# Two token blocks take the feed-forward in two half passes, partial sums in DRAM, and the batches are paired differently

## The chip, the cores and the metric

The kernel runs on one core of a Trainium2 chip. Its time is device time in microseconds (us), the median of several executions. The engines are PE (TensorE, matrix products; PEld is its loading of weights), DVE (VectorE), ACT (ScalarE), POOL (GpSimd) and SP (SyncE). SP computes nothing here: it issues every DMA, in one queue and in program order.

## The reference

Attention with a relative-position bias over 4 batches, 8 heads, 576 positions and a head size of 64, and behind it a gated feed-forward on the 2304 tokens that come out:

```python
scores = scale * np.matmul(q, k.transpose(0, 1, 3, 2))
x = (psi_rel / psi_i)[..., None]           # logs of distance and of position
bias = np.maximum(x @ w1 + b1, 0.0) @ w2   # 32 hidden units, one value per head
scores = scores + bias.transpose(2, 0, 1)[None, :, :, :]
attn = softmax(scores)                     # over the last axis
x = np.matmul(attn, v)                     # then (B*S, H*D) = (2304, 512)
h = x @ w_in                               # (2304, 2048)
g = h * (1.0 / (1.0 + np.exp(-h)))
out = g @ w_out                            # (2304, 512)
```

`w_in` and `w_out` arrive as 64-bit floats, all else as 32-bit.

## The kernel before

**Attention.** The bias depends on the head and the two positions alone. It is made once, in 36 tiles, and stored to DRAM in five pieces (`bias_d`), one for each chunk of 128 query rows (the fifth has 64). Two heads make a pair (`hp`), so a batch has 4 pairs and 5 chunks. For each head and chunk PE makes the scores (lines 561, 552), DVE adds the bias and takes the row maximum in one instruction (line 568, with a short read of its accumulator behind it), ACT takes the exponential (line 575), PE transposes (line 584), DVE or ACT evicts (lines 590 and 595, through the helper on lines 270 and 272), and one `pv` group of PE multiplies by the values (line 483). Batch 0 goes chunk by chunk, 20 `pv` groups. The other batches go pair by pair with two visits each, chunks 0 and 1 and then 2 to 4: 24 more groups, so the last is the 44th. A visit pair needs 9 maxima of line 568 and gives 2 `pv` groups. The loop `for some in ((1, 2), (3,))` sets who shares bias loads: the dictionary `biases` is cleared once per pair of heads and tuple, so batches 1 and 2 read each piece of the bias once for both, and batch 3 reads all of it again.

**Feed-forward.** The 2304 tokens are 6 blocks of 384 (`TB`), the 2048 columns 16 tiles of 128 (`NF`). Block 0 needs batch 0 alone, block 1 needs batches 0 and 1. `split_x` loads a block's attention output (`x_d`) and the reciprocals of its row sums (`rec_d`), multiplies (line 614, on DVE or POOL) and splits each of four tiles into a high part and a rest (lines 618 and 622), which go through PE as three products. A step `ff_step` is one column tile: 12 matmuls of 384 columns into `hp` (line 633), tanh on ACT (line 638), the gate on DVE (line 642), a split again (lines 646 and 650), and 9 matmuls of 512 columns that add into three banks `acc` (line 656). Behind 16 steps the banks are halved into SBUF (lines 681 and 683) and stored to `out`.

**Weights.** Block 0 meets each column tile first. `prepare` loads a 64-bit tile of 512 KB, and `narrow` makes 32-bit floats of it: one operation on ACT (line 356) and four on DVE (lines 360, 364, 369, 374). Then it is split, by ACT (line 387) and by POOL or DVE (line 391). There are 32 such tiles, a `w_in` and a `w_out` for each step. The split `w_in` is stored to DRAM (`win_d`, line 666) and loaded again by the blocks 1 to 5 (line 671); `w_out` stays in SBUF.

**Order.** All of it is recorded as operations with an assumed cost and a due time, and the class `Plan` writes one order for each engine from these: at each moment a free engine takes the ready operation with the earliest due time whose buffers are to be had. So attention and feed-forward are woven on every engine, and each engine then runs its list strictly in that order. `LEAD` is how long after batch 0 block 0 falls due, `STEP` the spacing of the steps while attention still runs (10 us in block 0, 7 in the next), `DF` the spacing behind it.

Of the kernel before, what the change touches and what calls it, by code (L numbers as in the profile page):

```python
# [8 lines left out]
F32 = mybir.dt.float32  # L9
# [3 lines left out]
ALU = mybir.AluOpType  # L13
# [4 lines left out]
DM, DFF = 512, 2048  # L18
NT = B * S
NF = DFF // 128  # L20
NC = DM // 128
TB = 384
NBLK = NT // TB
# [4 lines left out]
T0, DC, B1, BD, GAP0, DF, WU = 16.0, (4.5, 3.0), 36.0, 2.6, 2.0, 4.3, 24  # L28


PACE, LEAD, STEP = (1.1, 1.6), 30.0, (10.0, 7.0)


def f(ap):
    return ap.bitcast(F32)
# [180 lines left out]
def attention_moe_kernel(ctx: ExitStack, tc: tile.TileContext, q, k, v, small, w_in, w_out, lut, ident_d, out):  # L216
    nc = tc.nc
    V, A, G, T, SP = nc.vector, nc.scalar, nc.gpsimd, nc.tensor, nc.sync
# [10 lines left out]
    dpool = ctx.enter_context(tc.tile_pool(name="dram", bufs=1, space=DRAM))  # L229
# [9 lines left out]
    win_d = [dpool.tile([128, 2 * DM], F32, name=f"win_d{i}") for i in range(NF)]  # L239
    win_b = [Buf(None) for _ in range(NF)]  # L240
    x_d = [dpool.tile([128, NC, TB], F32, name=f"x_d{i}") for i in range(NBLK)]
    x_b = [Buf(None) for _ in range(NBLK)]

    rec_d = dpool.tile([NC, 2, NBLK * TB], F32, name="rec_d")
# [32 lines left out]
    def op(kind, where, prio, reads=(), writes=(), shy=6.0):  # L277
        def add(fn):
            plan.op(kind, where, prio, fn, reads, writes, shy=shy)
            return fn  # L280
        return add

    def load(kind, prio, writes, fn, bytes, reads=(), plain=False):
        plan.op(kind, ("SP", 0.52 if plain else 0.7), prio, fn, reads, writes, bytes)
# [92 lines left out]
    def prepare(t0, src):  # L377

        w, wr = buf("w", [128, DM]), buf("G", [128, 2, DM], F32R)
        if wide:  # L380
            narrow(t0, w, src)
        else:
            load("ld_w32", t0 - 6, [w], lambda e: SP.dma_start(out=tl(w), in_=src), 262144)

        @op("split_hi", ("ACT", 0.62), t0 + 0.5, reads=[w], writes=[(wr, 0)])
        def _(e):
            copy(e, tl(wr)[:, 0, :], tl(w))

# [235 lines left out]

    PAIRS = ((0, 0), (0, 1), (1, 0))

    def ff_step(blk, fi, xs, wr, acc, t0):
        hp, th, gg = bank("h", 1), buf("th", [128, TB]), buf("M", [128, 2, TB], F32R)
        for cc in range(NC):
            @op("h_mm", ("PE", 0.53), t0 + 0.01 * cc, reads=[xs[cc], wr], writes=[hp])  # L630
            def _(e, cc=cc):
                for m, (x, y) in enumerate(PAIRS):
                    T.matmul(out=tl(hp)[:, 0:TB], lhsT=tl(wr)[:, x, 128 * cc:128 * cc + 128], rhs=tl(xs[cc])[:, y, :],  # L633
                             start=(cc + m == 0), stop=(cc == NC - 1 and m == 2))

        @op("tanh", ("ACT", 0.5), t0 + 2.3, reads=[hp], writes=[th])
        def _(e):
            A.activation(out=tl(th), in_=tl(hp)[:, 0:TB], func=AF.Tanh, scale=0.5)  # L638

# [12 lines left out]
        for i in range(3):  # L652
            @op("out_mm", ("PE", 0.7), t0 + 2 * DF + 0.01 * i, reads=[gg, wo[fi]], writes=[acc[i]])
            def _(e, i=i):
                for m, (x, y) in enumerate(PAIRS):
                    T.matmul(out=tl(acc[i]), lhsT=tl(gg)[:, x, 128 * i:128 * i + 128], rhs=tl(wo[fi])[:, y, :],  # L656
                             start=(fi == 0 and m == 0), stop=(fi == NF - 1 and m == 2))

    def ff_block(blk, t0, step):
        xs = split_x(blk, t0 - 8)  # L660
        acc = [bank("acc", 1) for _ in range(3)]
        for fi in range(NF):
            t = t0 + step * fi
            if blk == 0:
                wr = prepare(t - 5, w_in[fi])
                load("st_in", t - 1, [win_b[fi]], lambda e, wr=wr, fi=fi: SP.dma_start(out=win_d[fi], in_=f(tl(wr).rearrange("p a n -> p (a n)"))), 524288, reads=[wr])
                if wo[fi] is None:
                    wo[fi] = prepare(t - 2, w_out[128 * fi:128 * fi + 128, :])
            else:
                wr = buf("G", [128, 2, DM], F32R)  # L670
                load("ld_in", t - 8, [wr], lambda e, wr=wr, fi=fi: SP.dma_start(out=f(tl(wr).rearrange("p a n -> p (a n)")), in_=win_d[fi]), 524288, reads=[win_b[fi]])
            ff_step(blk, fi, xs, wr, acc, t)
        for i in range(3):
            ob = buf("M", [128, DM])
            t = t0 + step * (NF - 1) + 2 * DF + 3
            cuts = [(0, DM)] if blk < NBLK - 1 or i < 2 else [(0, DM // 2), (DM // 2, DM)]
            for x, y in cuts:
                @op("out_ev", {"ACT": 0.18 + (y - x) * 0.00083, "DVE": 0.15 + (y - x) * 0.00104}, t, reads=[acc[i]], writes=[(ob, x)])
                def _(e, i=i, ob=ob, x=x, y=y):
                    if e == "ACT":  # L680
                        A.activation(out=tl(ob)[:, x:y], in_=tl(acc[i])[:, x:y], func=AF.Copy, scale=0.5)
                    else:
                        V.tensor_scalar_mul(out=tl(ob)[:, x:y], in0=tl(acc[i])[:, x:y], scalar1=0.5)

                row = TB * blk + 128 * i
                load("st_out", t + 1, [], lambda e, ob=ob, row=row, x=x, y=y: SP.dma_start(
                    out=out[row:row + 128, x:y], in_=tl(ob)[:, x:y]), 512 * (y - x), reads=[(ob, x)])


    kv, vs, sq = {}, {}, {}  # L690
    t = T0
# [11 lines left out]

    t1 = t + LEAD
    t2 = t1 + NF * STEP[0]
    for some in ((1, 2), (3,)):
        for hp in range(4):
            biases.clear()
            for b in some:
                pace = PACE[t > t2]  # L710
                kv, vs, sq = keys(b, hp, t), values(b, hp, t), sums(t)
                for chunks in ((0, 1), (2, 3, 4)):
                    t = visit(b, hp, chunks, kv, vs, sq, t, pace)
                factors(b, hp, sq, t)
    wo = [None] * NF
    for blk in range(NBLK):
        step = STEP[0] if blk == 0 else STEP[1] if t1 < t else DF
        ff_block(blk, t1, step)
        t1 += NF * step

    def warm_up():

# [65 lines left out]
```

## Time and profile before

| what | us |
|---|---|
| median of 3 runs (735.53 to 736.71) | 736.17 |
| the profiled execution's own time | 736.04 |
| its span | 734.3 |
| PE busy | 712.6 |
| DVE busy | 421.0 |
| ACT busy | 389.4 |
| POOL busy | 281.4 |

The own time is 1.7 us over the span, which is what lies ahead of the first and behind the last instruction. Matmuls overlap in the records, so a PE shown as busy may still give less than it can; what a piece of PE work costs at the least is read from an unbroken run of it in the chain of waits. Records of DVE overlap too: the instructions of one stretch, summed, give some 0.06 us per instruction more than DVE's busy time there.

### The profile page before, as it was taken

The numbers are of one execution on the slowest core, as the hardware profiler recorded it, in microseconds if no ns is written. First come the engines' busy times: TensorE is split into PE (matmuls) and PEld (weight loads), VectorE is DVE, ScalarE is ACT, GpSimd is POOL, SyncE is SP. The second block draws the span as 40 slices with busy tenths as digits, with TensorE's granted clock in tenths as the row PEclk, the third lists the DMA queues.
The fourth block names the chain that finished last, engine by engine and source line by source line (L and its number), as shares of the span: only waits on it lengthen the run. The fifth ranks groups of instructions, "written<-read, shape, count | busy, mean of one in ns | idle before, by whom it ended". The sixth has DMA issues, their size and how long they took to land.

```text
span 734.3 us, 13019 instructions
## 1 busy us (share of the span) xinstructions
PE 712.6 (97%) x4642; PEld 590.1 (80%) x4642; DVE 421.0 (57%) x862; ACT 389.4 (53%) x820; POOL 281.4 (38%) x277
## 2 busy tenths in 40 slices
PE   9899999999999999989999999999999999999997
PEld 4376698677777787778888888899998999999996
DVE  6999968999999999996553544213211221211111
ACT  8899968886786777765443454222222232222222
POOL 5464524474746445573122251123223322422221
PEclk9999999999999999999999999999999999999999
DMA  6998899898584594879856567736454644346001
GB/s 195 372 315 270 277 310 359 278 289 297 191 290 157 203 303 149 272 257 311 293 165 224 168 217 241 263 115 196 148 162 153 186 150 152 125 136 195 1 0 44
DMA packets 68384, 154.77 MB, mean 211 GB/s; under 512 B 9056, under 2 KB 24032, under 8 KB 68320
## 3 DMA queue, kind: packets, MB, share of 16 engines
q1 hardware_dynamic: 68320, 153.94, 63.7%
q8 instruction: 37, 0.61, 0.4%
q14 instruction: 27, 0.22, 0.1%
HBM read 125.12 MB, written 28.79 MB: 210 GB/s over the span
## 4 chain that ended last, share of the span: by engine, by line
PE 46%; issue 7%; DVE 3%; POOL 2%; DMA 1%; ACT 0%; POOLq 0%; DVEq 0%; ACTq 0%
PE psum L633 18%; PE psum L656 18%; PE psum L483 3%; PE psum L561 3%; PE psum L584 3%; POOL M L275 2%; DVE G L568 1%; DVE w L369 1%; DMA G<-in_k_dram 1%; PE psum L552 1%; DVE M L275 0%; DVE w L374 0%; DVE th L642 0%; DVE M L272 0%; DVE w L360 0%
## 5 line engine op out<-in xcount | busy, mean ns | idle before, releaser
L633 PE MATMUL psum<-M,G 128*128 128x384 f32 x1152 | 238.8, 339 | 1.0 <-POOL M L275 0.8
L656 PE MATMUL psum<-G,M 128*128 128x512 f32 x864 | 238.0, 397 | 1.2 <-DVE M L275 0.9
L633 PEld LDWEIGHTS psum<-M,G 128*128 128x128 f32 x1152 | 203.4, 188 | 16.6 <-POOL M L275 1.0
L275 POOL TENSOR_TENSOR M<-th,M 128x384 fp32r<-128x384 f32 x82 | 84.9, 1035 | 272.0 <-ACT M L270 189.3
L642 DVE SCALAR_TENSOR_TENSOR th<-th,psum 128x384 f32<-128x384 f32 x96 | 53.0, 552 | 216.4 <-ACT th L638 216.4
L656 PEld LDWEIGHTS psum<-G,M 128*128 128x128 f32 x864 | 156.7, 188 | 22.2 <-DVE M L275 1.6
L575 ACT ACTIVATE G<-G,sm 128x576 f32<-128x576 f32 (+1 forms) x144 | 111.8, 777 | 53.6 <-DVE sm L568 52.3
L638 ACT ACTIVATE th<-psum 128x384 f32<-128x384 f32 x96 | 47.1, 491 | 161.1 <-PE psum L633 160.0
L568 DVE CUSTOM_DVE_ANT_0 G<-psum,G 128x576 f32<-128x576 f32 (+1 forms) x144 | 106.5, 758 | 27.9 <-PE psum L561 15.5
L584 PE MATMUL psum<-ident,G 128*128 128x128 f32 x656 | 93.5, 276 | 5.7 <-DVE sm L568 3.3
L561 PE MATMUL psum<-G,M 128*128 128x288 f32 x512 | 90.9, 310 | 4.9 <-DVE sm L568 3.5
L584 PEld LDWEIGHTS psum<-ident,G 128*128 128x128 f32 x656 | 75.3, 141 | 23.0 <-issue 4.8
L561 PEld LDWEIGHTS psum<-G,M 128*128 128x128 f32 x512 | 73.9, 190 | 19.7 <-issue 6.7
L483 PE MATMUL psum<-pt,M 128*64 128x128 f32 (+3 forms) x880 | 87.5, 346 | 1.6 <-DVE sm L568 0.8
L483 PEld LDWEIGHTS psum<-pt,M 128*64 128x64 f32 x880 | 52.1, 137 | 30.7 <-issue 6.8
L270 ACT ACTIVATE pt<-psum 128x512 f32<-128x512 f32 (+3 forms) x111 | 59.4, 551 | 28.1 <-PE psum L584 27.0
L275 POOL TENSOR_TENSOR M<-M 64x256 fp32r<-64x256 f32 (+3 forms) x40 | 48.6, 1217 | 57.9 <-DVE M L272 21.0
L270 ACT ACTIVATE M<-th 128x384 fp32r<-128x384 f32 x81 | 42.3, 523 | 40.9 <-DVE th L642 40.0
L272 DVE COPY pt<-psum 128x512 f32<-128x512 f32 (+3 forms) x81 | 45.4, 571 | 21.8 <-PE psum L584 19.1
L275 POOL TENSOR_TENSOR G<-w,G 128x512 fp32r<-128x512 f32 x25 | 35.6, 1425 | 23.8 <-ACT G L270 19.9
L275 POOL TENSOR_TENSOR G<-G 128x576 fp32r<-128x576 f32 x21 | 32.2, 1540 | 29.6 <-PE psum L334 9.6
L326 ACT ACTIVATE G<-lut_sb,cb 128x528 f32<-128x528 f32 (+16 forms) x71 | 41.6, 662 | 0.0
(55 smaller groups left out, 574.1 us busy)
## 6 DMA issues: line engine op xcount, KB each, us to landing
G<-win_d SPq DMA_DIRECT2D x80, 512.0 KB
G<-bias_d SPq DMA_DIRECT2D x48, 576.0 KB
bias_d<-G SPq DMA_DIRECT2D x36, 295.5 KB
G<-in_k_dram SPq DMA_DIRECT2D x16, 576.0 KB
G<-in_w_in_dram SPq DMA_DIRECT2D x16, 512.0 KB
G<-in_w_out_dram SPq DMA_DIRECT2D x16, 512.0 KB
win_d<-G SPq DMA_DIRECT2D x16, 512.0 KB
M<-in_v_dram SPq DMA_DIRECT2D x16, 320.0 KB
```

The costliest lines, as they stand in the source:

```text
L270: A.activation(out=out, in_=in_, func=AF.Copy)
L272: ENG[e].tensor_copy(out=out, in_=in_)
L275: ENG[e].tensor_tensor(out=out, in0=in0, in1=f(in1), op=ALU.subtract)
L483: T.matmul(out=tl(o)[x, 0:w], lhsT=tl(vs)[:, (s + 1) % 5 * 128 + 64 * a:(s + 1) % 5 * 128 + 64 * a + 64], rhs=tl(pt)[:, s + 5 * a if s < 4 ...
L561: T.matmul(out=s[:, hf, 0:288], lhsT=tl(qs)[:, x0 + 128 * a:x0 + 128 * a + 128], rhs=tl(part)[:, S * a + 288 * hf:S * a + 288 * hf + 288], ...
L568: V.tensor_tensor_reduce(out=mine(p, a).rearrange("p (a n) -> p a n", a=2), in0=tl(sps[a]).rearrange("p (a n) -> p a n", a=2)[:, :, 0:widt ...
L575: A.activation(out=mine(p, a), in_=mine(p, a), func=AF.Exp, scale=-1.0, bias=tl(sm)[:, i + a:i + a + 1], accum_out=tl(sq)[:, 2 * c + a:2 * ...
L584: T.transpose(out=tl(tp)[:, 128 * s:128 * s + 128], in_=tl(p)[:, 128 * (s0 + s):128 * (s0 + s) + 128], identity=ident)
L633: T.matmul(out=tl(hp)[:, 0:TB], lhsT=tl(wr)[:, x, 128 * cc:128 * cc + 128], rhs=tl(xs[cc])[:, y, :], start=(cc + m == 0), stop=(cc == NC - ...
L638: A.activation(out=tl(th), in_=tl(hp)[:, 0:TB], func=AF.Tanh, scale=0.5)
L642: V.scalar_tensor_tensor(out=tl(th), in0=tl(th), scalar=1.0, in1=tl(hp)[:, 0:TB], op0=ALU.add, op1=ALU.mult)
L656: T.matmul(out=tl(acc[i]), lhsT=tl(gg)[:, x, 128 * i:128 * i + 128], rhs=tl(wo[fi])[:, y, :], start=(fi == 0 and m == 0), stop=(fi == NF - ...
```

## The change

Blocks 0 and 1 take the columns in two halves, by turns: block 0 with tiles 0 to 7, block 1 with tiles 0 to 7, block 0 with 8 to 15, block 1 with 8 to 15. A first half ends by storing its three halved accumulators to DRAM (`part_d`), a second half loads them (line 682 of the changed kernel) and adds them in its last eviction, on DVE alone. Each half calls `split_x` for itself. The second half of block 0 prepares its weight tiles with due times up to 40 us (`AHEAD`) earlier than its steps, and loads `w_in` back from `win_d` like the others. Blocks 2 to 5 are as they were. Of the attention, batch 1 now goes alone and batches 2 and 3 share the bias loads.

```diff
+AHEAD = 40.0
...
+    part_d = [dpool.tile([TB, DM], F32, name=f"part_d{i}") for i in range(2)]
+    part_b = [Buf(None) for _ in range(2)]
...
-                             start=(fi == 0 and m == 0), stop=(fi == NF - 1 and m == 2))
+                             start=(fi == fs[0] and m == 0), stop=(fi == fs[-1] and m == 2))
...
-        for fi in range(NF):
-            t = t0 + step * fi
-            if blk == 0:
-                wr = prepare(t - 5, w_in[fi])
-                load("st_in", t - 1, [win_b[fi]], lambda e, wr=wr, fi=fi: SP.dma_start(out=win_d[fi], in_=f(tl(wr).rearrange("p a n -> p (a n)"))), 524288, reads=[wr])
-                if wo[fi] is None:
-                    wo[fi] = prepare(t - 2, w_out[128 * fi:128 * fi + 128, :])
-            else:
+        for n, fi in enumerate(fs):
+            t = t0 + step * n
+            ahead, fresh = AHEAD if part else 0.0, wo[fi] is None
+            if wo[fi] is None:
+                wr = prepare(t - 5 - ahead, w_in[fi])
+                load("st_in", t - 1 - ahead, [win_b[fi]], lambda e, wr=wr, fi=fi: SP.dma_start(out=win_d[fi], in_=f(tl(wr).rearrange("p a n -> p (a n)"))), 524288, reads=[wr])
+                wo[fi] = prepare(t - 2 - ahead / 2, w_out[128 * fi:128 * fi + 128, :])
+            if part or not fresh:
                 wr = buf("G", [128, 2, DM], F32R)
...
+            if part:
+                load("ld_part", t - 12, [ob], lambda e, ob=ob, at=at: SP.dma_start(out=tl(ob), in_=at), 262144, reads=[(part, i)])
...
+                    if part:
+                        V.scalar_tensor_tensor(out=tl(ob)[:, x:y], in0=tl(acc[i])[:, x:y], scalar=0.5, in1=tl(ob)[:, x:y], op0=ALU.mult, op1=ALU.add)
...
+                if len(fs) < NF and not part:
+                    load("st_part", t + 1, [(part_b[blk], i)], lambda e, ob=ob, at=at: SP.dma_start(out=at, in_=tl(ob)), 262144, reads=[(ob, x)])
...
-    for some in ((1, 2), (3,)):
+    for some in ((1,), (2, 3)):
...
-    for blk in range(NBLK):
-        step = STEP[0] if blk == 0 else STEP[1] if t1 < t else DF
-        ff_block(blk, t1, step)
-        t1 += NF * step
+    low, high = range(NF // 2), range(NF // 2, NF)
+    runs = [(0, low, STEP[0], None), (1, low, STEP[1], None), (0, high, STEP[0], part_b[0]), (1, high, STEP[1], part_b[1])]
+    for blk, fs, step, part in runs + [(blk, range(NF), None, None) for blk in range(2, NBLK)]:
+        step = step or (STEP[1] if t1 < t else DF)
+        ff_block(blk, t1, step, fs, part)
+        t1 += len(fs) * step
```

The plan weaves anew from there on, so each engine's order moves. The three places below are those that the prediction speaks of. Most lines of the changed kernel are numbered 3 higher than before (483 is 486, 568 is 571, 633 is 636, 656 is 659, 459 is 462).

On PE, behind the 23rd `pv` group (the first row of the first piece). Before, the first feed-forward step (line 633) starts there:

```order
L483 MATMUL psum<-pt,M 64x256 x10
L584 MATMUL psum<-ident,G 128x128 x5
L561 MATMUL psum<-G,M 128x288 x4
L633 MATMUL psum<-M,G 128x384 x3
L552 MATMUL psum<-G,M 128x320 x2
L552 MATMUL psum<-G,M 128x256 x2
L552 MATMUL psum<-G,M 128x320 x2
L552 MATMUL psum<-G,M 128x256 x2
L633 MATMUL psum<-M,G 128x384 x9
```

In the changed kernel it starts behind the 24th, which is the fourth row from the end here:

```order
L587 MATMUL psum<-ident,G 128x128 x5
L564 MATMUL psum<-G,M 128x288 x4
L587 MATMUL psum<-ident,G 128x128 x4
L564 MATMUL psum<-G,M 128x288 x4
L528 MATMUL psum<-ident,sq 128x128
L587 MATMUL psum<-ident,G 128x128 x5
L486 MATMUL psum<-pt,M 64x320 x10
L587 MATMUL psum<-ident,G 128x128 x4
L636 MATMUL psum<-M,G 128x384 x12
L587 MATMUL psum<-ident,G 128x128 x5
```

The first step moved behind one more `pv` group, and both groups belong to batch 1 now. From the 26th to the 36th group more feed-forward stands between two groups than before: ahead of the 36th, 19 steps of line 633 against 17.

On DVE, around the 79th to the 81st maximum of line 568, in the fifth visit pair behind batch 0. Before, weight tiles (`w`, lines 360, 364, 369, 374) stand between the maxima:

```order
L369 SCALAR_TENSOR_TENSOR w<-G,w 128x512
L568 ISA G,sm<-psum,G 128x576
L568 ISA sm 128x1
L374 SCALAR_TENSOR_TENSOR w<-G,w 128x512
L568 ISA G,sm<-psum,G 128x576
L568 ISA sm 128x1
L360 TENSOR_SCALAR w<-w 128x512
L272 COPY pt<-psum 128x4x128
L364 TENSOR_SCALAR w<-w 128x512
L369 SCALAR_TENSOR_TENSOR w<-G,w 128x512
L272 COPY pt<-psum 128x5x128
L642 SCALAR_TENSOR_TENSOR th<-th,psum 128x384
```

Now there are none here; the eviction of a partial sum (line 693) and the tokens of the next half (`xp`) stand in their place:

```order
L571 ISA G,sm<-psum,G 128x576
L571 ISA sm 128x1
L617 TENSOR_TENSOR xp<-xp 128x384
L571 ISA G,sm<-psum,G 128x576
L571 ISA sm 128x1
L275 CAST M<-xp 128x384
L571 ISA G,sm<-psum,G 128x576
L571 ISA sm 128x1
L693 TENSOR_SCALAR M<-psum 128x512
L275 COPY xo<-psum 128x256
L275 COPY pt<-psum 128x4x128 x2
L275 CAST M<-xp 128x384
```

The weight tiles moved behind: before, all 32 are done ahead of the last maximum of the 36th `pv` group (the 108th); now 27 are done there, and the 32nd stands right behind the last maximum of the 38th group (the 117th).

On SP, where the last visits of batch 0 end. Before, the loads of the 64-bit weights and of `k` stand there with one piece of the bias (`G<-bias_d`):

```order
L352 DMA G<-in_w_out_dram 128x1024
L352 DMA G<-in_w_in_dram 128x1024
L497 DMA x_d_121<-xo 128x128
L352 DMA G<-in_w_out_dram 128x1024
L532 DMA rec_d<-rt 4x2x128
L534 DMA rec_d<-rt 2x1x64
L406 DMA G<-in_k_dram 128x1152
L459 DMA G<-bias_d_99 128x2x576
```

In the changed kernel:

```order
L462 DMA G<-bias_d_101 128x2x576
L462 DMA G<-bias_d_102 128x2x576
L355 DMA G<-in_w_in_dram 128x1024
L535 DMA rec_d<-rt 4x2x128
L500 DMA x_d_121<-xo 128x64
L537 DMA rec_d<-rt 2x1x64
L355 DMA G<-in_w_out_dram 128x1024
L409 DMA G<-in_k_dram 128x1152
L462 DMA G<-bias_d_99 128x2x576
L500 DMA x_d_121<-xo 128x64
L459 DMA G<-bias_d_103 64x576 x2
```

The bias of batch 1's second pair of heads moved in, which batch 2's visits used to put off: up to the 23rd `pv` group there are 40 issues of bias loads against 33.

## Rows read from the trace of the kernel before

**Rows 1.** The page: busy time of the engines over the whole span (its part 1), and from its part 2 the busy tenths of PE, of DVE and of the DMA engines in 40 slices of 18.4 us.

```profile
PE 712.6 (97%) x4642; PEld 590.1 (80%) x4642; DVE 421.0 (57%) x862; ACT 389.4 (53%) x820; POOL 281.4 (38%) x277
...
PE   9899999999999999989999999999999999999997
...
DVE  6999968999999999996553544213211221211111
...
DMA  6998899898584594879856567736454644346001
```

**Rows 2.** Busy time by stretch (the windows view). Columns: stretch in us, its length, then busy us (and instructions) of PE, PEld, DVE, ACT and POOL, the granted TensorE clock as a share of full speed, the mean busy share of the 16 DMA engines, GB/s.

```profile
90.00:145.90 55.90, 53.37 (x542) 45.62 (x532) 45.76 (x117) 42.85 (x98) 22.10 (x34) 1.00 0.97 319
145.90:219.80 73.90, 68.82 (x447) 56.25 (x446) 72.21 (x129) 56.52 (x118) 41.16 (x37) 1.00 0.79 266
219.80:334.60 114.80, 108.69 (x713) 88.55 (x712) 108.99 (x199) 84.28 (x179) 62.29 (x53) 1.00 0.68 229
334.60:464.40 129.80, 129.80 (x821) 109.78 (x820) 65.42 (x145) 58.23 (x128) 34.50 (x36) 1.00 0.71 231
361.60:464.40 102.80, 102.80 (x644) 87.26 (x643) 48.33 (x109) 44.75 (x100) 26.57 (x31) 1.00 0.64 208
464.40:734.30 269.90, 265.73 (x1332) 238.25 (x1331) 49.06 (x92) 67.34 (x132) 73.48 (x73) 1.00 0.41 131
```

**Rows 3.** The timeline of PE at three places: where the 23rd, the 36th and the 38th `pv` group (line 483) start. Columns: start us, us, engine, line, operation, tiles, shapes, count. A group is 10 instructions of the program and 20 of the trace.

```profile
145.85 2.38 PE L483 MATMUL psum<-pt,M 128*64 128x256 f32 x20
...
334.64 1.57 PE L483 MATMUL psum<-pt,M 128*64 128x320 f32 x10
...
361.62 2.91 PE L483 MATMUL psum<-pt,M 128*64 128x320 f32 x20
```

**Rows 4.** The chain of work that ended last, in order of time, inside the attention stage and just behind it: start us, us, what. Each row is a run of matmuls without a break, so its second column is what that piece costs on a PE that never waits.

```profile
334.71 2.84 PE psum L483 x20
337.56 1.14 PE psum L584 x9
338.69 1.06 PE psum L561 x8
...
345.97 2.31 PE psum L483 x20
...
351.68 1.06 PE psum L552 x8
...
475.93 2.10 PE psum L633 x12
478.03 2.08 PE psum L656 x9
```

**Rows 5.** DVE's instructions from 145.9 to 334.6 us by line and tile. Columns: line, operation, tiles, shapes, count, then busy us and mean ns of one, then DVE's idle time just before them and what ended it.

```profile
L568 DVE CUSTOM_DVE_ANT_0 G<-psum,G 128x576 f32<-128x576 f32 (+1 forms) x61 | 45.1, 755 | 1.7 <-PE psum L561 1.1 <-ACT G L575 0.3
L369 DVE SCALAR_TENSOR_TENSOR w<-G,w 128x512 uint32<-128x512 uint32 x29 | 30.0, 1035 | 0.4
L374 DVE SCALAR_TENSOR_TENSOR w<-G,w 128x512 uint32<-128x512 uint32 x30 | 27.0, 899 | 0.1
L360 DVE TENSOR_SCALAR w<-w 128x512 f32<-128x512 f32 x28 | 20.0, 713 | 0.8 <-ACT w L356 0.7
L364 DVE TENSOR_SCALAR w<-w 128x512 uint32<-128x512 uint32 x28 | 18.0, 642 | 0.2
...
L642 DVE SCALAR_TENSOR_TENSOR th<-th,psum 128x384 f32<-128x384 f32 x16 | 8.7, 547 | 2.0 <-ACT th L638 2.0
L275 DVE TENSOR_TENSOR G<-w,G 128x512 fp32r<-128x512 f32 x6 | 7.6, 1273 | 0.2 <-ACT G L270 0.2
L568 DVE DVE_READ_ACCUMULATOR2_ANT sm<- 128x1 f32 x61 | 4.8, 79 | 0.0
...
L275 DVE TENSOR_TENSOR M<-th,M 128x384 fp32r<-128x384 f32 x4 | 3.9, 996 | 0.0
...
L272 DVE CAST M<-th 128x384 fp32r<-128x384 f32 x6 | 2.9, 483 | 0.0
...
L272 DVE COPY xo<-psum 128x256 f32<-128x256 f32 (+1 forms) x3 | 1.3, 437 | 0.0
L275 DVE TENSOR_TENSOR M<-M 64x704 fp32r<-64x704 f32 x1 | 1.0, 1029 | 0.0
...
L614 DVE TENSOR_TENSOR xp<-xp 128x384 f32<-128x384 f32 x1 | 0.5, 549 | 0.0
```

**Rows 6.** The same stretch and engine with different shapes kept apart: two rows that the view before has merged.

```profile
L272 DVE COPY pt<-psum 128x512 f32<-128x512 f32 x9 | 6.1, 681 | 0.9 <-PE psum L584 0.9
...
L272 DVE COPY pt<-psum 128x640 f32<-128x640 f32 x7 | 5.7, 812 | 0.0
```

**Rows 7.** Two of DVE's four weight operations over the whole run (the view of one source line): count, shortest/median/longest ns, first and last start in us, shape.

```profile
L360 DVE TENSOR_SCALAR w<-w x32: 406/422/1920, 127.3 to 314.2; 128x512 f32<-128x512 f32 x32
...
L369 DVE SCALAR_TENSOR_TENSOR w<-G,w x32: 674/692/2218, 130.4 to 318.1; 128x512 uint32<-128x512 uint32 x32
```

**Rows 8.** What DVE waited for on the DMA side (the list of waits, whole run): us in total, times, longest us.

```profile
DVE xp L614 <- DMA xp<-x_d: 7.5, 4, 2.5
```

**Rows 9.** POOL's two operations on the tokens of a feed-forward block, from 145.9 to 334.6 us, columns as in rows 5.

```profile
L614 POOL TENSOR_TENSOR xp<-xp 128x384 f32<-128x384 f32 x7 | 8.8, 1264 | 4.8 <-DMA xp<-x_d 4.3 <-DMA xp<-rec_d 0.4
L275 POOL TENSOR_TENSOR M<-xp,M 128x384 fp32r<-128x384 f32 x7 | 8.3, 1197 | 2.1 <-DVE M L272 1.4 <-ACT M L270 0.4 <-PE psum L584 0.3
```

More of the change, by code (lines that the diff above doesn't have):

```diff
@@ L625, in attention_moe_kernel, with ff_step @@
     PAIRS = ((0, 0), (0, 1), (1, 0))
[L627 removed]
+    def ff_step(fs, fi, xs, wr, acc, t0):
         hp, th, gg = bank("h", 1), buf("th", [128, TB]), buf("M", [128, 2, TB], F32R)
@@ L656, in _, with ff_block @@
                     T.matmul(out=tl(acc[i]), lhsT=tl(gg)[:, x, 128 * i:128 * i + 128], rhs=tl(wo[fi])[:, y, :],
-                             start=(fi == 0 and m == 0), stop=(fi == NF - 1 and m == 2))
-    def ff_block(blk, t0, step):
+                             start=(fi == fs[0] and m == 0), stop=(fi == fs[-1] and m == 2))
+    def ff_block(blk, t0, step, fs, part=None):
         xs = split_x(blk, t0 - 8)
         acc = [bank("acc", 1) for _ in range(3)]
-        for fi in range(NF):
-            t = t0 + step * fi
-            if blk == 0:
-                wr = prepare(t - 5, w_in[fi])
-                load("st_in", t - 1, [win_b[fi]], lambda e, wr=wr, fi=fi: SP.dma_start(out=win_d[fi], in_=f(tl(wr).rearrange("p a n -> p (a n)"))), 524288, reads=[wr])
-                if wo[fi] is None:
-                    wo[fi] = prepare(t - 2, w_out[128 * fi:128 * fi + 128, :])
-            else:
+        for n, fi in enumerate(fs):
[6 more added lines that the diff above has]
+            if part or not fresh:
@@ L670, in ff_block @@
                 wr = buf("G", [128, 2, DM], F32R)
                 load("ld_in", t - 8, [wr], lambda e, wr=wr, fi=fi: SP.dma_start(out=f(tl(wr).rearrange("p a n -> p (a n)")), in_=win_d[fi]), 524288, reads=[win_b[fi]])
-            ff_step(blk, fi, xs, wr, acc, t)
+            ff_step(fs, fi, xs, wr, acc, t)
+        t = t0 + step * (len(fs) - 1) + 2 * DF + 3
         for i in range(3):
             ob = buf("M", [128, DM])
-            t = t0 + step * (NF - 1) + 2 * DF + 3
+            at = part_d[blk][128 * i:128 * i + 128, :] if len(fs) < NF else None
+            if part:
+                load("ld_part", t - 12, [ob], lambda e, ob=ob, at=at: SP.dma_start(out=tl(ob), in_=at), 262144, reads=[(part, i)])
@@ L676, in ff_block @@
             cuts = [(0, DM)] if blk < NBLK - 1 or i < 2 else [(0, DM // 2), (DM // 2, DM)]
             for x, y in cuts:
-                @op("out_ev", {"ACT": 0.18 + (y - x) * 0.00083, "DVE": 0.15 + (y - x) * 0.00104}, t, reads=[acc[i]], writes=[(ob, x)])
+                @op("out_ev", ("DVE", 0.15 + (y - x) * 0.00104) if part else {"ACT": 0.18 + (y - x) * 0.00083, "DVE": 0.15 + (y - x) * 0.00104},
+                    t, reads=[acc[i]], writes=[(ob, x)])
                 def _(e, i=i, ob=ob, x=x, y=y):
-                    if e == "ACT":
+                    if part:
+                        V.scalar_tensor_tensor(out=tl(ob)[:, x:y], in0=tl(acc[i])[:, x:y], scalar=0.5, in1=tl(ob)[:, x:y], op0=ALU.mult, op1=ALU.add)
+                    elif e == "ACT":
@@ L685, in ff_block @@
                 row = TB * blk + 128 * i
-                load("st_out", t + 1, [], lambda e, ob=ob, row=row, x=x, y=y: SP.dma_start(
-                    out=out[row:row + 128, x:y], in_=tl(ob)[:, x:y]), 512 * (y - x), reads=[(ob, x)])
+                if len(fs) < NF and not part:
+                    load("st_part", t + 1, [(part_b[blk], i)], lambda e, ob=ob, at=at: SP.dma_start(out=at, in_=tl(ob)), 262144, reads=[(ob, x)])
+                else:
+                    load("st_out", t + 1, [], lambda e, ob=ob, row=row, x=x, y=y: SP.dma_start(
+                        out=out[row:row + 128, x:y], in_=tl(ob)[:, x:y]), 512 * (y - x), reads=[(ob, x)])
     kv, vs, sq = {}, {}, {}
```

## The prediction

> **What bounds the kernel now.** I read the page first. PE is busy 712.6 of 734.3 us [rows 1], so time can be won only where that busy time is not full: the busy tenths show DVE at 8 to 9 in the first 18 slices and falling from there, PE without a gap behind them. The windows say it more sharply [rows 2]. From 145.9 to 334.6 us DVE is busy 72.21 + 108.99 = 181.2 of 188.7 us; from 334.6 on PE is busy in every microsecond and DVE in half of them. I chose these two cuts because `pv` groups start there, the 23rd and the 36th [rows 3]: just behind the 23rd the feed-forward begins, and at the 36th the last of the 32 weight tiles has been made. The chain of waits prices PE's work where nothing interrupts it [rows 4]: 12 matmuls of line 633 take 2.10 us, 9 of line 656 2.08, 8 of line 561 or of line 552 1.06, 9 transposes 1.14, a `pv` group 2.31 (256 columns) or 2.84 (320). By these, PE's order holds 170 us of work between the 23rd and the 36th group (192 of line 633, 153 of 656, 212 of 561, 48 of 552, 264 of 584, 13 groups), so PE could have been done 18 us sooner. That is all there is to win. What fills DVE there is attention's maxima, 45.1 us, and the weight tiles, 30.0 + 27.0 + 20.0 + 18.0 = 95.0 us [rows 5].
>
> So the end is DVE's queue up to the last weight tiles, and then PE's work that is left. Before: 334.6 us and 734.3 - 334.6 = 399.7 us.
>
> **The change part by part.** The matmuls are the same in number. Weight tiles too: 32, one each. What changes is how much PE work stands in the order beside DVE's work. In the changed order DVE's heavy stretch ends at the 38th group (its 117th maximum), with the 32nd tile right behind it; there are two numbers to work out, DVE's work up to there and PE's work from there.
>
> *DVE.* I counted its order between the 49th maximum (the last that the 23rd group needs) and the 108th before, the 117th after. Each mean is reduced by 0.06 us, since records overlap by that much. Added [rows 5, 6]: 9 maxima with their accumulator reads, 9 x (0.755 + 0.079 - 0.12) = 6.4; evictions for the transposed weights, 6 of 512 and 5 of 640 elements, 6 x 0.62 + 5 x 0.75 = 7.5; 8 casts of 384, 8 x 0.42 = 3.4; 5 evictions of `pv`, 1.9; subtractions on line 275, 3 of 384, 2 on `M` of 64 partitions, and 2 fewer on weights, 2.8 + 1.9 - 2.4 = 2.3; 4 gates, 1.9; two block ends and two multiplications of tokens (line 614) at about 0.5 each, 2.0. Removed: five of the weight operations (2, 1, 1, 1 of lines 360, 364, 369, 374), 3.7. The sum is +21.7, so 181.2 + 21.7 = 202.9 us of DVE work.
>
> *DVE's pace.* It was busy 97.7% of the first part of its stretch (72.21 of 73.9) and 94.9% of the second (108.99 of 114.8) [rows 2]; in the second PE was busy 94.7%, in the first 93.1%. The changed stretch has more PE work beside the same DVE work, which is nearest to the second part, so I take 94.9%: 202.9 / 0.949 = 213.8 us. The 38th group then starts at 145.9 + 213.8 = 359.7 us, where before the 36th started at 334.6 and the 38th at 361.6 [rows 3].
>
> *PE from there.* Behind the start of the 38th group the changed order has less than the old one behind its 36th: 48 matmuls of line 633 (8.4 us), 36 of 656 (8.3), 24 of 561 (3.2), 8 of 552 (1.1), 32 transposes (4.0) and two `pv` groups (5.15), 30.2 us by rows 4. That leaves 399.7 - 30.2 = 369.5 us. The last 270 us are PE alone, with DVE at 49.06 [rows 2], and nothing of the change reaches them.
>
> *Sum.* 359.7 + 369.5 = 729.2 us of span, 730.9 with the 1.7 us around it. The profiled execution stands 0.13 below the median of the runs, so I say 731.
>
> *Partial sums.* The last evictions of the two second halves (6) read PSUM and SBUF on DVE, like the gate: 512 elements against its 384. Two thirds longer at most than 0.547 us, 0.9, and not below a gate; three of them are in a row at a block's end. They come behind the 38th group, where DVE has room (48.33 busy of 102.8 us [rows 2]), so they cost nothing; without that room, 6 x 0.9 = 5.4 us. The same holds for the 8 extra reloads of `w_in` and the stores and loads of the partials: SP issues them where the DMA engines are busy 0.64 to 0.79 [rows 2]. An in-order store that waits for an eviction holds up whatever load stands behind it in SP's queue, a price that this trace does not separate; from 0 to the longest wait of DVE for tokens, 2.5 us each [rows 8], for four block ends. I take 0, as loads are issued several visits ahead, and keep 10.0 as the other end.
>
> *Tokens split twice.* Each half calls `split_x`. Two of the extra multiplications on DVE were priced above; when DVE has one, it may also wait for the load: 7.5 us in four times over the run, so 1.9 each [rows 8]. Between 0 and 3.8; I take 0, since the only such operation in the stretch did not wait [rows 5], and the pace holds 5% of idle time.
>
> *POOL.* Ten more of its token operations fall in the stretch, at 1.264 and 1.197 us [rows 9]: 12 us on top of 41.16 + 62.29 = 103.4 [rows 2]. A DVE operation beside POOL's can be long: line 360 takes 422 ns in the median and up to 1920, line 369 692 and up to 2218 [rows 7]. POOL's density would be (103.4 + 12) / 213.8 = 0.54 against 0.55, so the means above already hold this, and I add nothing.
> The Trainium skill, in "SBUF — State Buffer", section "Who interferes with whom", says that DVE and GpSimd share one pair of ports as an exclusive lock, taken by whoever issues first, and that the other blocks for the whole instruction. By that rule what counts is which operations meet, not the density. The spread of line 360 in rows 7 agrees with a block. What it would add at most is a rival below.
>
> **The rivals.**
>
> *DVE keeps the faster pace.* At 97.7% the stretch takes 202.9 / 0.977 = 207.7 us and the time is 725; with no idle time at all, 720. For it: fewer weight tiles are due just in time. Against it: with PE nearly full as well, each waits for the other more often.
>
> *No change.* If both engines' pace falls a little below the second part's (DVE at 93%: 218.2 us) the time is 735 to 736. The old stretch had 18 us of slack on PE; the changed one has 170 + 30.2 = 200.2 us of PE work in 213.8, which is 94%, and no row shows both that full over 200 us. At PE's old 170 / 188.7 = 90% it would take 222 us and the time would be 739.
>
> *Slower: the DMA queue at the end of batch 0.* Batch 1 alone needs its second pair's bias at once, 7 more issues up to the 23rd group, 3.3 MB with 0.1 of other loads. From 90 to 145.9 us the DMA engines are already 97% busy at 319 GB/s [rows 2]. 3.4 MB take 10.7 us at that rate, and there is room for 3% of 55.9, 1.7 us. If attention or the first weight tiles wait for all of it, everything behind moves by 9.0 us, and the time is 740. It decides when the loads that are pushed back are the ones that DVE needs next; the order shows the first feed-forward step behind one more `pv` group, which speaks for it. Against it: DVE was busy only 45.76 of those 55.9 us, so something else had slack too, and loads run ahead of their use.
>
> *Slower: POOL's lock.* If each of the ten extra POOL operations stops DVE for its whole length, 12 us are added on DVE's path: 743. Against it: over the stretch the long weight operations exceed their medians by about a third of a microsecond each, on 115 operations beside 103 us of POOL, so a POOL microsecond has cost DVE some 0.3, not 1.
> By the Trainium skill's rule (the same page and section) the full block is the price of each meeting; the trace agrees that meetings are costly, not that each operation meets one.
>
> **How the numbers follow.** The forecast case (727 to 734.7): 0.42. The faster pace (below 727): 0.15. No change: 0.15. Slower: 0.28, of which the DMA queue has 0.15, PE that cannot be that full 0.10 and POOL's lock 0.03. A measurement of this kernel tells 0.2% from nothing, so faster is below 734.7, slower above 737.6: 0.57, 0.15, 0.28. The range runs from a DVE that never idles (720) to POOL's lock or the DMA queue with a block end or two on top (745).
>
> **What would show it.** Right: the 38th `pv` group near 360 us and the end some 370 us behind it; DVE 94 to 96% busy from the 23rd to the 38th group; PE's unbroken stretch from there on. The DMA rival would show as a 23rd or 26th group later than before by 5 us or more (before, 145.9 for the 23rd), with DVE or PE idle until a bias or weight load. POOL's lock would show in longer means of lines 360 to 374. The forecast is wrong if PE has gaps behind the 38th group, or if DVE's busy share from the 23rd to the 38th falls under 93%.

## The result and the profile after

The changed kernel takes 744.55 us (median of 4 runs, 742.73 to 746.13) against 736.18 for the kernel before beside it: 1.0113 times the old time, with a 95% interval of 1.0088 to 1.0138. It is slower, by 8 us, where 5 us faster was forecast. The profiled execution is the fastest of the four and has a span of 740.9 us. Two of the experiments below had one execution in a slow state each (1395.31 us in half_bias_before, 992.64 in plan_half_before), which their medians leave out.

The page of the changed kernel, the same rows as [rows 1]:

```profile
PE 714.4 (96%) x4642; PEld 589.8 (80%) x4642; DVE 433.0 (58%) x882; ACT 385.6 (52%) x818; POOL 292.2 (39%) x289
...
PE   9899999897999999999999999999999999999997
...
DVE  7998968999987698999766464313212211211111
...
DMA  6999899989865998699557647844554645336001
```

PE's matmuls are as many as before and nearly as long (714.4 against 712.6 us). Of the 6.6 us by which the span grew, 4.8 are therefore gaps on PE and 1.8 longer matmuls. DVE has 12 us more to do, POOL 11. DVE's tenths of 7 and more now reach to the 20th slice, two further than in [rows 1].

Next, PE's timeline where the 23rd, the 36th and the 38th `pv` group start, as in [rows 3], and the windows between those places and the 28th group (230.3) and the 44th (471.2), columns as in [rows 2]:

```profile
148.21 2.38 PE L486 MATMUL psum<-pt,M 128*64 128x256 f32 x20 [0.26 <-ACT rt L273]
...
343.93 2.37 PE L486 MATMUL psum<-pt,M 128*64 128x320 f32 x16
...
370.37 2.91 PE L486 MATMUL psum<-pt,M 128*64 128x320 f32 x20
```

```profile
90.00:148.20 58.20, 53.97 (x531) 45.62 (x529) 47.20 (x114) 43.21 (x100) 23.36 (x34) 1.00 0.99 341
148.20:230.30 82.10, 75.20 (x471) 60.94 (x471) 77.93 (x140) 58.19 (x124) 44.61 (x42) 0.98 0.84 289
230.30:343.90 113.60, 108.64 (x708) 89.22 (x707) 98.04 (x185) 72.58 (x157) 57.62 (x52) 1.00 0.83 283
343.90:370.40 26.50, 24.88 (x167) 20.02 (x166) 22.28 (x45) 16.40 (x35) 10.24 (x10) 1.00 0.64 206
370.40:471.20 100.80, 100.21 (x634) 84.66 (x633) 59.25 (x126) 47.31 (x105) 34.28 (x32) 1.00 0.66 217
471.20:740.90 269.70, 265.65 (x1332) 238.21 (x1331) 48.11 (x92) 67.32 (x132) 73.70 (x73) 1.00 0.41 134
```

The last 270 us are the same as before, and from the 38th group on PE is full again (100.21 of 100.80). The loss lies ahead of it: the 38th group starts at 370.4, where 361.6 was before. Between the 23rd and the 38th group DVE is busy 77.93 + 98.04 + 22.28 = 198.25 of 222.2 us, 89.2%, falling from 94.9 over 86.3 to 84.1% over the three parts. The whole stretch from the 23rd to the 38th group in one window, first before and then in the changed kernel:

```profile
145.90:361.60 215.70, 204.51 (x1335) 167.33 (x1334) 198.28 (x364) 154.28 (x324) 111.37 (x95) 1.00 0.75 253
```

```profile
148.20:370.40 222.20, 208.72 (x1344) 170.17 (x1344) 198.25 (x368) 147.16 (x315) 112.47 (x102) 0.99 0.81 276
```

DVE does the same amount of work in both, 198.3 us. Before, it was busy 91.9% of the stretch, now 89.2%, and the stretch is 6.5 us longer.

What DVE waited for between the 26th and the 38th group (the list of waits of DVE from 202 to 370.4 us: us in total, times, longest us; four of its rows), and the costliest of its work from 148.2 to 370.4, columns as in [rows 5]:

```profile
DVE pt L275 <- PE psum L587: 5.3, 8, 1.3
DVE M L275 <- POOL xp L617: 4.1, 2, 3.4
DVE sq L518 <- ACT G L578: 2.1, 2, 1.1
DVE G L571 <- PE psum L564: 2.0, 4, 0.7
```

```profile
L571 DVE CUSTOM_DVE_ANT_0 G<-psum,G 128x576 f32<-128x576 f32 (+1 forms) x67 | 50.1, 757 | 3.2 <-PE psum L564 2.0 <-PE psum L555 0.7 <-issue 0.2
L372 DVE SCALAR_TENSOR_TENSOR w<-G,w 128x512 uint32<-128x512 uint32 x28 | 25.4, 907 | 0.3
L377 DVE SCALAR_TENSOR_TENSOR w<-G,w 128x512 uint32<-128x512 uint32 x28 | 23.1, 824 | 0.3
...
L363 DVE TENSOR_SCALAR w<-w 128x512 f32<-128x512 f32 x27 | 17.9, 663 | 1.7 <-ACT w L359 1.5
L367 DVE TENSOR_SCALAR w<-w 128x512 uint32<-128x512 uint32 x27 | 17.1, 634 | 0.2
```

DVE idles in front of evictions of PE's transposes and behind POOL's tokens, a little at a time. Its operations themselves are no longer than before: 757 ns against 755 for a maximum, 907 and 824 against 1035 and 899 for the two long weight operations [rows 5].

### The profile page after: what moved, and what is told of

The parts are those of the page before. It is cut to its first block, busy times and chain, and to the rows that moved or that the text cites. A ratio compares the mean times of both kernels' runs of the same rounds, so it can differ in the third digit from the quotient of the medians.

```text
span 740.9 us, 13154 instructions
## 1 busy us (share of the span) xinstructions
PE 714.4 (96%) x4642; PEld 589.8 (80%) x4642; DVE 433.0 (58%) x882; ACT 385.6 (52%) x818; POOL 292.2 (39%) x289
## 4 chain that ended last, share of the span: by engine, by line
PE 67%; DMA 11%; issue 10%; DVE 7%; POOL 3%; SPq 1%; ACT 1%; POOLq 0%; DVEq 0%; ACTq 0%
PE psum L659 20%; PE psum L636 20%; PE psum L486 8%; PE psum L587 7%; PE psum L564 7%; PE psum L337 4%; POOL M L278 3%; DMA G<-bias_d 3%; DMA G<-in_w_in_dram 2%; DMA win_d<-G 2%; DMA G<-in_w_out_dram 1%; PE psum L738 1%; DMA G<-in_k_dram 1%; DMA xp<-x_d 1%; PE psum L555 1%
## 5 line engine op out<-in xcount | busy, mean ns | idle before, releaser
L278 POOL TENSOR_TENSOR M<-th,M 128x384 fp32r<-128x384 f32 x84 | 87.7, 1044 | 240.9 <-ACT M L273 177.1
L273 ACT ACTIVATE pt<-psum 128x640 f32<-128x640 f32 (+3 forms) x112 | 56.7, 524 | 34.3 <-PE psum L587 31.8
L275 DVE COPY pt<-psum 128x512 f32<-128x512 f32 (+3 forms) x80 | 49.1, 618 | 22.3 <-PE psum L587 18.4
L278 POOL TENSOR_TENSOR M<-M 64x256 fp32r<-64x256 f32 (+3 forms) x37 | 42.8, 1161 | 46.9 <-DVE M L275 14.1
L273 ACT ACTIVATE M<-th 128x384 fp32r<-128x384 f32 x74 | 38.7, 524 | 40.4 <-DVE th L645 40.3
L278 POOL TENSOR_TENSOR G<-G 128x576 fp32r<-128x576 f32 x22 | 35.2, 1612 | 26.5 <-PE psum L337 9.7
```

What stands on the lines that cost most here:

```text
L273: A.activation(out=out, in_=in_, func=AF.Copy)
L275: ENG[e].tensor_copy(out=out, in_=in_)
L278: ENG[e].tensor_tensor(out=out, in0=in0, in1=f(in1), op=ALU.subtract)
```

## The experiments

The kernel has a planner that weaves all engines' instructions anew whenever one of its numbers changes. That makes two kinds of experiments: those that keep an order and change what an instruction does, and those that change the plan. The expectations name their theories by letters: A is the pairing of the batches together with weight tiles that the half passes bunch late, B the bytes of the extra transfers, C the order that the plan writes, D the load on the DMA queue, E DVE's extra work, F the due times of the weight tiles, G the weaving itself, and H a worth of the old pairing that doesn't depend on the weaving.

**Each part alone.**

```diff
-    for some in ((1, 2), (3,)):
+    for some in ((1,), (2, 3)):
```

> Batch 1 alone, batches 2 and 3 sharing the bias, no half passes. Its order up to the 28th pv group has the feed-forward steps and the weight tiles at the same places as in the changed kernel. Theory A (two places lose: the new pairing starts the feed-forward late and loses some 8 us of PE work between 125 and 190 us, and the half passes bunch the weight tiles late and lose some 5 us between 340 and 400): 742 to 746 us, the 28th group near 230 as in the changed kernel, no loss behind 340. Theory B (the extra 10 MB of transfers of the half passes slow everything): within 2 us of before, 736 to 738, since the pairing moves bias loads and adds none.

The kernel before with this line took 744.97 us (1.0118, 1.0098 to 1.0137): as much as the whole change loses, with none of the extra transfers of theory B. The opposite edit, the changed kernel with the old pairing:

> Half passes with the old pairing (batches 1 and 2 together). Theory A: the stretch up to the 27th group as before (206 to 208 us, against 212 in the changed kernel), but the second half cannot start before batch 1 ends at the 34th group, so PE has no feed-forward between the 28th and the 34th and the time is 745 or more. Theory B: slow from the first extra transfers on, 744 to 748; the 27th group is the same in both theories, so what tells is where PE's work goes missing: in one gap between the 28th and 34th group (A) or all along (B).

It took 775.18 us (1.0518, 1.0491 to 1.0545). A window of it, columns as in [rows 2]:

```profile
251.00:302.50 51.50, 29.23 (x188) 21.66 (x186) 35.27 (x71) 26.64 (x57) 11.65 (x12) 0.77 0.58 194
```

Here the feed-forward stands still at its eighth step over six `pv` groups (the 29th to the 34th), since block 1's half needs tokens that this pairing makes later. PE is busy 29 of 51.5 us and is granted 0.77 of its clock. As woven here, the half passes need the new pairing; this run says nothing on their own cost.

**The lead of the weight tiles.** The number `AHEAD` of the changed kernel, 40, set to 0 and to 80:

```diff
-AHEAD = 40.0
+AHEAD = 0.0
```

> The changed kernel with AHEAD 0, so the second-half weight tiles fall due with their steps. The 17th to 32nd tile move later on DVE (the last behind maximum 126 instead of 119). Theory A: the late bunch grows, 747 to 752. Theory B: same bytes, 743 to 746.

> The changed kernel with AHEAD 80: the 17th to 32nd tile are spread from the 72nd to the 111th maximum, into the stretch from 220 to 300 us where DVE was idle 14%. Theory A: the loss between 340 and 400 us goes, some 5 us, and the loss before 190 stays: 738 to 741. Theory B: same bytes, 743 to 746.

745.88 (1.0132, 1.0108 to 1.0157) and 747.77 (1.0156, 1.0133 to 1.0179). Neither brought back what was lost, and preparing earlier was no better than not preparing ahead at all. The 738 to 741 us that theory A expected of `AHEAD` 80 did not come.

**The bytes of the bias.** All larger loads of the bias, those that the pairing adds among them, are made half as large, with the order of every engine unchanged. The second head adds the first head's bias, so the result is that of another bias.

```diff
-                out=tl(bias), in_=bias_at(c, 15, [dims[0], None, dims[1]], 2 * hp, 2)), 589824, reads=[bias_b[c]])
+                out=tl(bias)[:, 0:S], in_=bias_at(c, 15, [None, *dims], 2 * hp, 1)), 589824, reads=[bias_b[c]])
```

> The kernel before, with each load of the bias for the chunks 0 to 3 cut to one head's half (the second head's rows add the first head's bias, so that computation is changed); every engine's order is as before. A control for the next two. Theory D (the DMA queue at the end of batch 0 is what the new pairing pays for): 733 to 736. Theory C (the order itself costs it: the plan puts the first feed-forward step one pv group later, whatever the transfers really take): 734 to 737.

> The new pairing alone, with the same halved bias loads, order as in pairing_alone. Theory D: the 8 us go, within 3 us of half_bias_before, and the DMA share between 120 and 200 us falls under 0.9. Theory C: 6 to 9 us above half_bias_before, with the first feed-forward step still near 163 us.

> The changed kernel with the same halved bias loads. Theory D: 1 to 7 us under half_bias_before, since the half passes gained 7 us between 190 and 340 and gave some back later. Theory C: as the changed kernel, 742 to 745.

Measured: 736.15 (0.9989, 0.9976 to 1.0002), 744.29 (1.0102, 1.0076 to 1.0127) and 744.39 (1.0098, 1.0069 to 1.0127). Half of those bytes are gone, and the loss stays. A window of half_bias_pairing in the stretch where its first feed-forward step is late:

```profile
160.00:170.00 10.00, 8.84 (x56) 6.09 (x58) 10.00 (x15) 6.85 (x13) 7.96 (x6) 1.00 0.57 190
```

The DMA engines are busy 0.57 there (0.91 in the pairing with full loads), and DVE all of the time. The first step starts at 163.92 us, against 164.09 with full loads. So the bytes in the queue are not the cause; the order of the issues in SP's queue was the same in both.

The reverse of it, six more loads of that size in the old order, between the 17th and the 23rd group:

```diff
+            SP.dma_start(out=spare[extra].rearrange("p a n -> a p n"), in_=bias_at(0, 15, [None, [BW + 15, 128], [1, S]], 0, 2))
```

> The kernel before with six extra transfers of 576 KB (3.5 MB, DRAM to DRAM, used by nothing) put into SP's queue between the 17th and 19th pv group, where the new pairing puts its seven extra bias loads; all else in the old order. Theory D: 740 to 746. Theory C: within 2 us of before.

It took 802.97 us (1.0899, 1.0862 to 1.0935), far above either expectation, and is no test of them. I had sent the loads from DRAM to DRAM, to leave SBUF as it was. A part of the timeline of SP's queue (start, us) shows what that does:

```profile
124.34 0.68 SPq L733 DMA_DIRECT2D spare<-bias_d  x1
125.14 11.13 SPq L352 DMA_DIRECT2D G<-in_w_out_dram  x1
136.31 0.71 SPq L733 DMA_DIRECT2D spare<-bias_d  x1
137.37 11.42 SPq L352 DMA_DIRECT2D G<-in_w_in_dram  x1
```

The load behind each of these two transfers stands 11 us in SP's queue. Behind the other four, the next instruction of the queue stands 5.05, 12.48, 11.09 and 11.23 us. From 140 to 150 us no engine works, with the DMA engines at 0.18 (63 GB/s), columns as in [rows 2]:

```profile
140.00:150.00 10.00, 0.00 (x0) 0.00 (x0) 0.00 (x0) 0.00 (x0) 0.00 (x0) 0.50 0.18 63
```

**What the plan believes.** If the order, not the transfers, makes the loss, a planner that is told that these loads are half as large should weave the pairing more tightly. The transfers stay whole.

```diff
-..., 2 * hp, 2)), 589824, reads=[bias_b[c]])
+..., 2 * hp, 2)), 294912, reads=[bias_b[c]])
```

> The new pairing alone, with all transfers in full, but the plan is told half the bytes for the four larger bias loads (294,912 instead of 589,824). Its order then has three feed-forward steps by the 24th pv group instead of none, as before the change (two). Theory C (the loss is the order that the plan writes when it believes the DMA queue is full): 735 to 739, with PE's loss up to 200 us back to that of before. Theory D (the queue really is full there, so the earlier steps would only wait for their loads): 742 to 746.

> The changed kernel with the same false byte count in the plan, all transfers in full. Up to the 27th group its order is like plan_half_pairing, from the 28th on like the changed kernel. Theory C: the early loss of 8 us goes: 735 to 738, and the half passes still bring nothing, since what they gain before 340 us is given back behind it. Theory D: 742 to 746.

> Control: the kernel before with the same false byte count in the plan. Its order barely changes around batch 0's end. Both theories: 735 to 739.

Measured: 748.63 (1.0168, 1.0149 to 1.0186), 743.5 (1.0105, 1.0074 to 1.0137; its six executions spread from 738.58 to 748.25) and, for the control, 746.21 (1.0146, 1.0131 to 1.0160). All three lie above what theory C expected, and only the 743.5 lies in D's 742 to 746. The first step of the pairing now starts at 153.65 us, 10 us earlier, and the kernel is no faster. The control is the run that turned the study: the old kernel, doing its old work, lost 10 us from being woven anew. Together with it ran the test of E, the changed kernel of this set with the token work taken off DVE:

```diff
-            @op("x_mul", {"DVE": 0.6, "POOL": 1.15}, t - 0.1, reads=[xr], writes=[xb])
+            @op("x_mul", ("POOL", 1.15), t - 0.1, reads=[xr], writes=[xb])
```

(and likewise `x_hi` on ACT alone and `x_lo` on POOL alone).

> plan_half_after with the token splits of the feed-forward taken from DVE (line 614 on POOL alone, the high part on ACT alone, the rest on POOL alone). DVE has some 8 us less work in the stretch. Theory E (the half passes win nothing because their own DVE work, 12 us more over the run, eats what the better mix gives): 729 to 734. Rival F (what they lose at the end is a matter of when weight tiles fall due, not of DVE's amount of work): within 2 us of plan_half_after.

746.07 (1.0137, 1.0124 to 1.0151): no gain, so E has no support. This run is woven anew too, so it doesn't show that DVE's extra work costs nothing.

**The same work, woven anew.** Three numbers of the plan are each moved by a few per cent in both kernels, one at a time. No instruction is added or taken away by the text; the planner may give a few that either of two engines can do to the other one.

```diff
-    LATE = 4.0
+    LATE = 4.1
...
-                        dma = max(dma, end + 0.65) + nbytes / 340e3
+                        dma = max(dma, end + 0.65) + nbytes / 345e3
...
-PACE, LEAD, STEP = (1.1, 1.6), 30.0, (10.0, 7.0)
+PACE, LEAD, STEP = (1.1, 1.6), 31.0, (10.0, 7.0)
```

> The kernel before with one number of the plan moved a little (LATE 4.0 to 4.1 us), so that the same work is woven into another order. Theory G (the old order is an unusually good one, and any other weave of the same work leaves DVE idle more before the last weight tile): 739 to 747. Theory H (the old pairing and whole blocks are better in themselves, and small changes of the weave don't matter): within 2 us of before.

> The changed kernel with the same small move (LATE 4.1). Theory G: a spread around the changed kernel and around the rewoven old ones, 738 to 748. Theory H: within 2 us of the changed kernel, 742.5 to 746.5.

> The kernel before with another small move (the plan's DMA rate 340 to 345 GB/s). Theory G: 739 to 747, and DVE idle before the last weight tile over 9 us against 6.2. Theory H: within 2 us of before.

> The changed kernel with the plan's DMA rate at 345 GB/s. Theory G: 738 to 748. Theory H: within 2 us of the changed kernel.

> The kernel before with LEAD 31 in place of 30, a third weave of the old work. Theory G: 739 to 747, near the two rewoven ones (742.9 both). Theory H: within 2 us of before.

> The changed kernel with LEAD 31. Theory G: 738 to 748, and over the three pairs the changed kernel and the old work stand within 2 us of each other. If the change has a cost of its own, the changed weaves stand above the old ones by 3 us or more.

| weave | kernel before, us | ratio (95%) | changed kernel, us | ratio (95%) |
|---|---|---|---|---|
| as given | 736.18 | 1 | 744.55 | 1.0113 (1.0088 to 1.0138) |
| a, `LATE` | 742.86 | 1.0084 (1.0064 to 1.0105) | 743.24 | 1.0096 (1.0069 to 1.0124) |
| b, DMA rate | 742.86 | 1.0089 (1.0065 to 1.0113) | 741.93 | 1.0068 (1.0049 to 1.0087) |
| c, `LEAD` | 747.36 | 1.0151 (1.0130 to 1.0171) | 743.53 | 1.0083 (1.0056 to 1.0110) |

The ratios are all to the kernel before as given, run beside each. Without that one order, the old work takes 744.4 us in the mean of three weaves, and the changed work 743.3 in the mean of four; with plan_half_before and plan_half_after counted as further weaves it is 744.8 and 743.4. Theory H, within 2 us of each kernel as given, fails for the old one in all three weaves. Where the old order is better is seen on DVE, from 125 us to the end of the last weight tile (one window of each; first before, then four of other orders: rewoven_before_a, rewoven_before_b, rewoven_before_c, and the changed kernel as given):

```profile
125.00:319.50 194.50, 182.75 (x1225) 147.49 (x1225) 188.33 (x347) 147.02 (x309) 104.26 (x90) 1.00 0.72 243
```

```profile
125.00:327.90 202.90, 187.98 (x1246) 150.00 (x1246) 191.59 (x354) 146.54 (x307) 109.93 (x94) 1.00 0.67 232
```

```profile
125.00:327.90 202.90, 186.81 (x1229) 148.33 (x1229) 190.90 (x345) 145.57 (x308) 102.25 (x89) 0.99 0.69 232
```

```profile
125.00:332.20 207.20, 190.16 (x1254) 153.97 (x1254) 190.12 (x356) 146.56 (x311) 101.16 (x89) 0.98 0.69 234
```

```profile
125.00:374.50 249.50, 232.27 (x1527) 187.28 (x1527) 223.59 (x418) 167.64 (x361) 124.22 (x113) 0.99 0.83 284
```

DVE idles 194.50 - 188.33 = 6.2 us in the old order, 11.3, 12.0 and 17.1 in the three others of the same work, and it does 2 to 3 us more work up to the last tile there. So the last tile ends at 319.5 in the old order, 8.4 us later in a and b, and 12.7 later in c. Their runs took 6.4, 6.4 and 11.1 us more than the kernel before beside them. In the changed kernel DVE idles 25.9 us.

The same three weaves from the 23rd to the 38th group:

```profile
146.20:367.60 221.40, 206.50 (x1337) 167.25 (x1336) 197.09 (x363) 152.53 (x323) 115.81 (x99) 1.00 0.71 244
```

```profile
143.90:367.40 223.50, 207.24 (x1335) 167.38 (x1334) 199.58 (x367) 153.71 (x325) 105.50 (x95) 0.99 0.72 245
```

```profile
147.00:374.50 227.50, 208.82 (x1335) 171.11 (x1334) 194.56 (x371) 151.56 (x321) 108.84 (x95) 0.98 0.71 238
```

DVE is busy 89.0, 89.3 and 85.5% there, against 91.9% in the old order and 89.2% in the changed kernel.

A rival is TensorE's clock, which was granted in full in [rows 2] and at 0.98 in one window of the changed kernel. It is not needed for the loss: in rewoven_before_a the granted clock is 1.00 in both windows above, and that kernel lost 6.4 us.

No kernel tried beats the one before.

## Why the prediction was wrong

*What held.* PE's time from the 38th group: 369.5 forecast, 740.9 - 370.4 = 370.5 measured. The evictions of the partial sums and the extra reloads cost next to nothing behind the 38th group, as said: PE is busy 100.21 of 100.80 us there.

*The start.* The 23rd group came at 148.2 instead of 145.9, 2.3 us of the miss. That is less than the 5 us that the DMA rival asked for.

*The step that failed* is the one headed DVE's pace. It took 94.9% from the second part of the old stretch and 213.8 us; measured were 89.2% and 222.2 us, 8.4 more, and below the 93% that the prediction named as the sign of being wrong. With the start and 1.0 behind the 38th group that makes 2.3 + 8.4 + 1.0 = 11.7, the whole distance from 729.2 to 740.9. The median stands another 1.8 us above the profiled execution. I treated 94.9% as what this mix of work lets DVE reach. It was what one order reached, in a window that ended at the 36th group: up to the 38th the old order itself has 91.9%, with its weight tiles done by the 36th, and other weaves of the old work have 85.5 to 89.3%. Up to the last tile DVE idles 5.1 to 10.9 us more in these, and the time rises by 6.4 to 11.1 us. The forecast credited the change with the old order's luck, and none of the orders woven anew inherited it.

*A count that was off the other way.* DVE's work from the 23rd to the 38th group was forecast at 202.9 us, 21.7 more than in the old stretch; measured were 198.25, 17.1 more. The weight operations make the difference: the four took 25.4 + 23.1 + 17.9 + 17.1 = 83.5 us, where 95.0 - 3.7 = 91.3 was forecast, as their means were shorter; the rest came out some 3 us higher. At 94.9% the measured work would have taken 208.9 us, so the pace alone cost 13.3 us, and the work, by luck, gave 4.9 back. The trace also puts the last weight tile two maxima further back than the forecast did, behind the 119th, at 371.4 to 374.5 us. And it has 204 matmuls of line 633, 144 of line 656, 56 of line 552 and 274 transposes where the prediction counted 192, 153, 48 and 264 in PE's old stretch: 173 us in place of 170, so the slack was 15 us and not 18.

*What the half passes did.* PE's idle time by window, the length less its busy time, from 100 us on:

| PE idle, us | 100 to 180 | 180 to 340 | 340 to 400 |
|---|---|---|---|
| before, as given | 4.7 | 9.0 | 0.0 |
| old work, weaves a to c | 6.9 to 7.9 | 10.0 to 13.8 | 0.0 to 1.0 |
| changed kernel, as given | 8.7 | 6.2 | 3.4 |
| changed kernel, all four weaves | 8.4 to 10.5 | 5.9 to 7.3 | 1.8 to 4.1 |

So the changed kernel does idle less on PE between 180 and 340 us, where it has more feed-forward to do: that part of the idea worked. It idles more ahead of that, and that comes with the pairing (8.9 us in pairing_alone). The late first step is the likely reason, since the pairing idles only 5.9 us there when the plan is told of half the bytes and starts that step 10 us earlier; that run then lost more behind 180 us (12.2). It idles more again from 340 to 400, and this follows the time of the last weight tile: 2.5, 3.4 and 6.3 us with `AHEAD` 80, 40 and 0, with the last tile at 356, 374 and 395 us. The changed kernel's window from 230.3 to 343.9 suggests that DVE was no longer the one bound there: busy 86% beside a PE at 96%.

*The rivals.* The one that PE cannot be that full, at PE's old 90%, gave 222 us for the stretch and 739, and the stretch came out at 222.2. By the counts of the trace it is 203 us of PE work in 222.2, 91%, against 173 in 188.7, 92%, before. So PE's share stayed where it was, as this rival said, with a chance of 0.10; why it stays there no run shows. The DMA rival named 740, near the time, but not for its reason: half_bias_pairing and half_bias_after kept the loss with half of the bytes. POOL's lock would have shown in longer weight operations, and these were shorter than before, with 12 POOL operations more in the page. The Trainium skill, in "SBUF — State Buffer", section "Who interferes with whom", calls the shared ports an exclusive lock between DVE and GpSimd; no run here separates one such meeting, and the added operations left no trace in those means.

*What stays open.* The change's 1.1% need not be a price of its parts: the same work in other orders spans 742.9 to 747.4, and the changed work 741.9 to 744.6. The runs don't show why the old order packs DVE so well; that its planner's numbers were chosen for it would explain it, and was not tested. With three or four orders a side, a difference of 1 or 2 us between the two kinds of work can't be told. For the same reason the 744.97 of the pairing alone and the two values of `AHEAD` can't be put down to those edits: they lie inside what weaving alone does, or a little above it (747.36).

## What to carry to other kernels

The pace of an engine in an order that a planner wove belongs to that order, so don't carry it over to another. Before an edit that makes the planner weave anew is credited or blamed, weave the old kernel anew as well, by moving one of the plan's numbers by a few per cent, some three times: here that alone cost 0.8 to 1.5%, as much as the change. A forecast for such an edit should start from the middle of those orders, not from the best one.

## What the runs showed of the hardware

A transfer of 576 KB from DRAM to DRAM in SP's queue held up the next load of that queue for 11.13 and 11.42 us in the rows shown, with the DMA engines at 0.26 busy over 120 to 170 us. The kernel with six of them took 66 us longer. Whether the target in DRAM or the shape of the transfer does this was not separated.

TensorE's granted clock is 1.00 in all windows of [rows 2]. In the changed kernel the 0.98 from 148.2 to 230.3 us is one short stretch at the lower of the two levels, half the clock (1.2 of 2.4 GHz), behind gaps on PE, here in rows of 4 us:

```profile
156.00:160.00 4.00, 2.57 (x16) 1.81 (x14) 4.00 (x7) 3.44 (x12) 2.40 (x3) 0.93 0.61 207
160.00:164.00 4.00, 4.00 (x22) 1.79 (x20) 4.00 (x7) 2.83 (x6) 3.70 (x4) 0.65 0.93 322
164.00:168.00 4.00, 4.00 (x29) 3.54 (x25) 4.00 (x6) 2.85 (x6) 2.25 (x2) 1.00 0.99 372
```

The `pv` group of 320 columns that starts there, at 160.21 us, took 4.19 us, against 2.84 in [rows 4]. Such gaps don't always lower it: from 172 to 176 us PE is busy 2.52 of 4 us at 1.00. In halves_alone the clock is at the lower level, 0.50, from 280 to 305 us, where PE is busy 8.2 of 25 us.
